# A fourth token pair in the seven-product output projection of a fused attention-plus-gated-unit kernel

## The chip, the cores and the metric

The kernel runs on one core of one Trainium2 chip. The core has five engines that matter here: TensorE (PE in the profile, PEld its weight loads) multiplies matrices into PSUM, VectorE (DVE), ScalarE (ACT) and GpSimd (POOL) do the elementwise work, and SyncE (SP) only issues DMAs. Each engine works through its own queue in order, and waits where a semaphore says that an input isn't there yet. The metric is the device time of one execution in microseconds; before the change it is 214.34, the median of three runs (214.32 to 215.28).

## The reference

For 2,048 tokens of width 512, the kernel adds three terms: the input, a linear attention with learned feature maps (32 heads of 16), and a gated unit with 1,792 hidden columns. Both branches read the layer-normalised input.

```python
xn = _layernorm(x, axis=-1)
return x + _A_ref(xn, A_wqkv, A_w_phi, A_wo) + _B_ref(xn, B_w_gate, B_w_up, B_w_down)

# A: phi = [softmax(q @ w_phi), softmax(-(q @ w_phi))], the same for k
kv = einsum("bhsf,bhsd->bhfd", phi_k, v);  z = sum of phi_k over the tokens
o = (phi_q @ kv) / (phi_q . z + 1e-6);     A = o @ wo
# B
h = (xn @ w_gate) * (xn @ w_up);           B = h @ w_down
```

## The kernel before

The tokens are cut into 16 tiles of 128, and these into four groups T = 0 to 3 of four tiles. Each group has a tile `hT(T)` of hidden values, with the hidden columns on the partitions: 14 chunks of 128 by 512 tokens.

*Gated unit, first half.* Group 0 is computed plainly: the steps `g` and `u` (14 each, lines 348 and 437) are four matmuls of 512 columns, `gc` copies the gate out of PSUM, `h` multiplies. Groups 2 and 3 together, and the two halves of group 1, are computed by block products (line 802): the product of a 2 by 2 block matrix of tokens with one of weights is made from seven products instead of eight, from sums of blocks made beforehand. `z` and `Nz` make the token sums, `t` the weight sums, `p1` to `p7` the products, `k1` to `k3` copy PSUM to SBUF, `j` and `d4` join them into hidden values; in odd blocks `m` multiplies gate by up. Steps with an `N` ahead belong to group 1 and have 256 columns, those without have 512.

*Attention.* For tile n, `vk` and `k` project to values and keys, `kx`/`ky` are the two exponentials on ScalarE, `kr` sums and `ki` inverts them on VectorE, `kp` multiplies on GpSimd, `kv` accumulates on TensorE; `q`, `qx` to `qp` are the same for queries. `qt` turns the result by a DMA, `ab` multiplies with the accumulated state, `de`, `rd`, `ot` divide, `oT` turns again by a DMA. `a` is the layer norm of one tile and `xt` the DMA that turns it; `wq` is the DMA that turns the query weights. All these DMAs are issued on SP, in one queue.

*Output projection.* A plain tile (`fin_steps`, line 662) takes nine steps `f` of two matmuls with 512 columns: 14 chunks of `hT` with `w_down`, and four of the attention output with `wo`; `fs` scales, adds the input, and `fo` stores. Tile 12 is cut by columns in 384 (`f12`) and 128 (`F12`). The six tiles 9, 10, 11 and 13, 14, 15 are instead taken in pairs (n, n + 4) by `pair_steps` (line 936): seven block products over seven chunks each, with 256 columns. Their token sums `S` (`hidden_sum`, line 925) are made on VectorE or GpSimd from `hT(2)` and `hT(3)`, three tiles (384 columns) at once. `P1a` to `P7b` are the products (four and three matmuls), `P2w`, `P3w`, `P8w`, `P4w` the attention part (four matmuls each), `K` the copies out of PSUM, `A` and `B` additions, `J` the last join that writes the output tile, `X` the store. `c` and `w` steps (`ct`, `cb`, `wt`) prepare `w_down`.

*What sets the order.* The whole order is written out by hand in the string `ORDER`, one word for each step; a suffix `/v`, `/g` or `/a` puts a step on VectorE, GpSimd or ScalarE. The loop at line 1060 issues the words one after the other. The string `SLOTS` names the buffer that each step takes out of its ring. `=k`, `=ab`, `=f` and `=ab2` change the use of the two PSUM banks that are not in the general ring of six; they serve here as marks. Between `=k` and `=ab` lie most of group 0 and the key side of the attention; between `=ab` and `=ab2` lie all block products of the gated unit; behind `=ab2` lie the pairs. The same loop adds a wait: after a VectorE step with both operands in SBUF (`z`, `t`, `S`, `m` and the like), the next GpSimd step waits until it is done.

Of the kernel before, what the change touches and what calls it, by code (L numbers as in the profile page):

```python
# [20 lines left out]
def _bcast_ap(ap_in: bass.AP, new_ap):  # L21
# [4 lines left out]
g3 gc3/a =k g1 gc1/a fk2 fk0 g0 u3 fkv2/v fkv0/v fka2/a fka0/a k1 ky1 kx1 u0 gc0/v h3 k0 u1 k2 h0 kr1 h1 ki1 kx0  # L26
ky0 kr0 s6 s5 ky2 n1.0 g4 g6 gc4/a u6 g7 n0.5 kx2 gc6/a gc7/a s7 k3 kp1/g s4 sc4 kx3 n1.6 n0.6 ky3 u7 h7 h6 a5/g
# [27 lines left out]
Np2.5 q10.0 Np4.4 m3.3/g k3.5/a Nk1.5/a p5.5 p4.5 Np6.5 Nj2.5 qi9 j7.5 Nm2.5/g t32/g d4.4/a Nd4.4/a Np5.4 Nj7.4
p1.6 Nk2.5/a Np7.5 Nk3.5/a q10.1 t33/v d4.5 Np3.4 wr2 Nj3.4 wf2 k1.6/a p3.5 Np4.5 up51/a Nd4.5 p6.6 Np1.6
Nk1.6/a Np2.6 qx10 j2.6 k2.6/a qp9/g j3.5 Np5.5 Nj7.5 m7.5/v m3.5/v t40/v t41/g q12.0 p5.6 Np6.6 q12.1 p7.6
Nk2.6/a Np3.5 Np7.6 Nj2.6 Nj3.5 qy10 wp2 qp13/g k3.6/a p1.7 p1.8 Nk3.6/a qx12 k1.7/a Np5.6 Np4.6 p2.7 j7.6 p3.6
p4.6 Nm7.5/g Nd4.6/a oT4 qr10 Nj7.6 Np1.7 qy12 p2.8 p6.7 Np3.6 k1.8/a Nk1.7/a j3.6 k2.7/a Np6.7 j2.7 Nk2.7/a
d4.6/a q14.0 q14.1 Np7.7 Nj3.6 j2.8 Np2.7 p7.7 Nk3.7/a qx14 Np2.9 Nm3.5/v m2.7/v t42/v Nj2.7 k3.7/a Np4.7 qy14  # L60
Np5.7 Nd4.7 p5.7 Nj7.7 t43/g Np2.8 Np1.8 p4.7 Np3.7 j7.7 Nm2.7/g Nm7.7/v Nj3.7 Nm3.7/v Nk1.8/a Np6.8 Nk2.8/a
p1.9 d4.7 p3.7 k1.9/a Np7.8 Np5.8 p6.8 m7.7/g qt13 fo3 qt8 j3.7 p2.9 Nk3.8/a Np4.8 Nd4.8/a k2.8/a p1.10 Nj7.8
Nj2.8 Np3.8 m3.7/g Np1.9 j2.9 Nk1.9/a k1.10/a t50/v ws2 Nj3.8 S1.0/g p6.9 p2.10 Nj2.9 j2.10 Np6.9 p7.8 Np5.9
p5.8 k2.9/a m2.9/v p7.9 Nk2.9/a t52/v k3.8/a j7.8 Np7.9 Nk3.9/a t51/g p5.9 p1.11 p4.8 Nj7.9 p3.8 k3.9/a p4.9
t53/g p6.10 Np4.9 Np3.9 Nm2.9/v j7.9 d4.8/a j3.8 m7.9/g qi10 k1.11/a Nd4.9 p6.11 p3.9 Nj3.9 up61/a t60/v d4.9
Nm7.9/g qp10/g k2.10/a Np1.11 p2.11 j3.9 p7.10 k2.11/a k3.10/a j2.11 Np1.10 p5.10 j7.10 Nm3.9/g m2.11/g m3.9/v
# [9 lines left out]
f4.3 Nj3.13 =ab2 ab8 qy11 ct2.3/g S0.1/v de8/v rd8 ot8 qi15 f4.7 f6.5 f5.2 Nm3.13/g f4.4 f5.0 ct2.0/g ab9 f7.5
S0.2/v Nm7.13/v S2.6/g de9/a rd9 ot9 S2.2/v S2.3/v F12.3 f6.6 f4.8 F12.1 f7.6 wt2.0/v S1.1/g S1.5/g qt14 qt10
qp15/g qt12 m7.13/v oT8 f4.0 j3.13 f7.3 f4.6 F12.2 f5.8 fs4 fs6 ab14 f5.7 de14/a ct1.1/a rd14 oT9 fo0 ot14
S0.6/v m3.13/v f5.1 f5.4 qr11 qi11 f8.8 oT14 f12.5 F12.6 f8.3 fs7 f5.5 f5.3 F12.5 f12.2 ab12 f8.2 P1b.10 de12/a
wt1.1/g wt2.2/g P1a.10 f5.6 f8.7 cb21.0/a f8.5 f8.4 F12.0 K1.10/v S2.1/v rd12 ot12 f12.6 qt15 fo6 P1a.11 f12.1  # L80
ab13 f12.4 P1b.11 oT12 qp11/g fs5 fo7 fo4 fo5 qt11 wt2.1/g ct3.0/a de13/a rd13 ot13 S1.2/v cb22.1/v S1.6/v f8.0
P1a.9 f12.0 P1b.9 f8.1 S3.0/v wt2.3/v S2.5/v wt4.1/v oT13 f12.3 F12.7 f12.7 f12.8 S3.6/v fs12 K1.11/a S2.0/v
ab10 F12.8 ct3.1/a F12.4 cb21.1/a de10/a K1.9/a A1.9/v wt3.1/v P6a.10 f8.6 wt4.0/g P6a.9 P6b.9 K6.9/a cb22.0/a
A6.9/g S3.5/g wt4.3/g S3.4/g P6a.11 P5a.10 P5b.10 Fs12 P6b.10 K6.10/a P2a.9 P2w.9 K5.10/a fs8 P5a.9 rd10 ot10
ab15 wt3.0/v P7a.9 P5b.9 P8w.10 fo12 fo8 oT10 Fo12 K5.9/a de15/v wt4.2/v P7b.9 P2b.9 J2.9 rd15 ot15 K7.9/a
P7a.10 P7b.10 P4w.9 P6b.11 S3.1/g K7.10/v P3b.9 P4a.9 P4b.10 P4w.10 ab11 B6.9/v A7.10/g oT15 K6.11/a A1.10/v
# [6 lines left out]
SLOTS = {  # L93
    "vt": "012341234",
    "s": (
        "012345120345120345120345120435102450321520512405314021341502135024310345243502145102135454351355"
        "425302541532024524343410323514235230251021324153450341245530305230145023201532"
    ),
    "x": (
# [20 lines left out]
def kernel(  # L120
# [896 lines left out]
    t0 = 1  # L1017
# [93 lines left out]
```

## Time and profile before

| | us |
|---|---|
| median of three runs | 214.34 |
| the profiled execution, its own time | 215.05 |
| its span, first to last instruction | 213.3 |
| mean granted TensorE clock (share of full) | 0.998 |

The profiled execution is 0.71 us above the median, and 1.75 us of its own time lie outside the span. In the rows of the profile a line reads: where in the code, engine, operation, output and inputs by name, shape and type, how often; then the busy time, the mean duration of one in nanoseconds, and the idle time of that engine just before, with what ended it. A chain row reads: start in us, length in us, what. A window row gives the busy time of each engine in that stretch, with the number of instructions in brackets.

### The profile page before, as it was taken

How to read it: one execution, taken by the hardware profiler on the slowest of the kernel's cores; microseconds unless marked ns; L12 is line 12 of the kernel's file. 1: busy time of each engine (PE TensorE's matmuls, PEld its weight loads, DVE VectorE, ACT ScalarE, POOL GpSimd, SP SyncE). 2: the span in 40 equal slices, each digit the busy share in tenths (PEclk: the TensorE clock that was granted, in tenths of full speed). 3: DMA queues.
4: the chain of work that ended last, by engine and by line, in shares of the span. 5: the costliest groups of instructions: out<-in, count | busy, mean ns of one | idle time of the engine just before them, and what ended most of it. 6: DMA issues, size and time to landing. Idle time of an engine off the chain costs nothing.

```text
span 213.3 us, 4174 instructions
## 1 busy us (share of the span) xinstructions
PE 206.5 (97%) x1452; PEld 117.8 (55%) x1452; DVE 185.3 (87%) x372; ACT 153.2 (72%) x296; POOL 149.8 (70%) x146
## 2 busy tenths in 40 slices
PE   8999999989999899989999999999999999999993
PEld 3555444444554454535656665655555555679983
DVE  5777799979899999979999999999879979796854
ACT  4648899979999799989989898686755502555200
POOL 3613577987897778997889876768868468909610
PEclk9999999999999999999999999999999999999999
DMA  5999999402314035773000001800000095452222
GB/s 158 260 274 383 379 297 177 92 8 33 70 25 77 0 68 105 147 103 77 0 3 0 0 3 32 179 13 3 0 0 0 0 130 119 101 148 75 50 78 74
DMA packets 47253, 19.95 MB, mean 94 GB/s; under 512 B 37504, under 2 KB 46976, under 8 KB 47104
## 3 DMA queue, kind: packets, MB, share of 16 engines
q1 hardware_dynamic: 47232, 19.69, 40.6%
q8 instruction: 11, 0.18, 0.4%
q14 instruction: 10, 0.08, 0.2%
HBM read 8.67 MB, written 2.10 MB: 50 GB/s over the span
## 4 chain that ended last, share of the span: by engine, by line
PE 78%; DMA 9%; DVE 6%; SPq 2%; ACT 1%; POOL 1%; issue 1%; DVEq 0%; ACTq 0%; POOLq 0%
PE sa L824 16%; PE fin L678 15%; PE sc L824 9%; PE k L337 5%; PE q L337 5%; PE da L960 5%; PE pv L337 4%; PE sb L824 4%; DMA wT<-in_A_wqkv_dram 3%; PE u L351 3%; DMA wgu<-in_B_w_up_dram 2%; PE g L351 2%; DMA oT<-otok 2%; PE db L960 2%; PE dd L960 2%; PE dc L960 2%
## 5 line engine op out<-in xcount | busy, mean ns | idle before, releaser
L549 DVE TENSOR_REDUCE sums<-e 128x64 f32<-128x1024 f32 x32 | 38.3, 1198 | 3.0 <-ACT e L537 2.9
L559 POOL TENSOR_TENSOR phik<-e,rs 128x1024 bf16<-128x1024 f32 x16 | 30.8, 1935 | 13.8 <-DVE rs L554 10.4
L678 PE MATMUL fin<-wd,hT 128*128 128x512 bf16 (+2 forms) x154 | 37.1, 359 | 0.0
L559 POOL TENSOR_TENSOR phiq<-e,rs 128x1024 bf16<-128x1024 f32 x16 | 31.5, 1975 | 4.8 <-DVE hT L846 2.7
L824 PEld LDWEIGHTS <-T 128*128 128x128 f16 x224 | 21.9, 98 | 17.4 <-issue 0.5
L846 POOL TENSOR_TENSOR hT<-u_sb,hT 128x256 f16<-128x256 bf16 (+1 forms) x23 | 21.1, 920 | 5.3 <-DVE T L774 3.0
L357 ACT COPY k<-sa 128x512 f32<-128x512 f32 (+1 forms) x42 | 19.5, 483 | 5.6 <-PE sa L824 4.1
L359 ACT ACTIVATE k<-sa 128x512 f32<-128x512 f32 (+1 forms) x41 | 19.7, 494 | 4.9 <-PE sa L824 4.2
L824 PEld LDWEIGHTS <-wgu 128*128 128x128 bf16 x168 | 16.3, 98 | 12.3
L337 PEld LDWEIGHTS <-x 128*128 128x128 f16 x144 | 13.4, 98 | 14.4 <-DMA x<-xn 1.1
L678 PEld LDWEIGHTS <-hT 128*128 128x128 f16 (+1 forms) x154 | 14.0, 98 | 11.8
L337 PE MATMUL pv<-vk,x 128*128 128x512 bf16 x48 | 18.2, 379 | 0.8 <-DMA x<-xn 0.8
L351 PEld LDWEIGHTS <-wgu 128*128 128x128 bf16 x128 | 12.0, 98 | 12.0 <-DMA wgu<-in_B_w_up_dram 0.4
L554 DVE RECIPROCAL rs<-sums 128x64 f32<-128x64 f32 x32 | 17.3, 543 | 1.5
L337 PE MATMUL k<-vk,x 128*128 128x512 bf16 x48 | 18.2, 379 | 0.0
L824 PE MATMUL sa<-ss,T 128*128 128x512 f16 x56 | 16.3, 379 | 0.0
L839 DVE SCALAR_TENSOR_TENSOR hT<-sc,k 128x512 f16<-128x512 f32 (+1 forms) x28 | 15.3, 548 | 1.1 <-PE sc L824 0.9
L359 ACT ACTIVATE wgu<-wgu,up 128x1024 bf16<-128x1024 bf16 x14 | 16.0, 1152 | 0.0
L710 ACT ACTIVATE junk<-wgu 128x1024 bf16<-128x1024 bf16 x14 | 15.0, 1077 | 1.2 <-DMA wgu<-in_B_w_gate_dram 1.2
L843 DVE TENSOR_TENSOR u_sb<-sc,k 128x512 bf16<-128x512 f32 (+1 forms) x28 | 15.0, 545 | 0.6 <-PE sc L824 0.5
L537 ACT ACTIVATE e<-q 128x512 f32<-128x512 f32 x24 | 13.9, 601 | 1.9 <-POOL phik L559 1.4
L351 PE MATMUL u<-xnT,wgu 128*128 128x512 bf16 (+1 forms) x64 | 14.6, 352 | 0.1
(160 smaller groups left out, 495.7 us busy)
## 6 DMA issues: line engine op xcount, KB each, us to landing
out_dram<-o_sb SPq DMA_DIRECT2D x15, 128.0 KB, 1.9
wd<-in_B_w_down_dram SPq DMA_DIRECT2D x1, 1792.0 KB, 15.4
wgu<-in_B_w_gate_dram SPq DMA_DIRECT2D x2, 640.0 KB, 7.0
wgu<-in_B_w_up_dram SPq DMA_DIRECT2D x2, 640.0 KB, 8.2
xall<-in_A_x_dram SPq DMA_DIRECT2D x1, 1024.0 KB, 12.1
xall<-in_A_x_dram SPq DMA_DIRECT2D x4, 128.0 KB, 2.5
vk<-in_A_wqkv_dram SPq DMA_DIRECT2D x2, 256.0 KB, 3.4
wgu<-in_B_w_gate_dram SPq DMA_DIRECT2D x2, 256.0 KB, 5.0
```

What stands on the lines that cost most here:

```text
L337: nc.tensor.matmul(ps, lhsT=xt(n)[:, j, :], rhs=w[:, j, :], start=(j == 0), stop=(j == DC - 1))
L351: nc.tensor.matmul(ps, lhsT=w[:, c, f * P:(f + 1) * P], rhs=xnT[:, c, lo:hi], start=(c == 0), stop=(c == DC - 1))
L357: A.copy(out=dst, in_=src)
L359: A.activation(out=dst, in_=src, func=AF.Identity, scale=scale)
L549: V.tensor_reduce(out=sums[:], in_=ev(), axis=AX.X, op=ALU.add)
L554: V.reciprocal(out=rs[:].rearrange("p a b -> p (a b)"), in_=held.pop((s + "s", n))[:])
L559: eng.tensor_tensor(out=phi[:].rearrange("p g (x f) -> p (g x) f", f=DH), in0=ev(), in1=held.pop((s + "i", n))[:].to_broadcast((P, 2 * H, ...
L678: nc.tensor.matmul(held["fin", n, lo], lhsT=l, rhs=r, start=len(done) == 1, stop=len(done) == FC + DC)
L824: nc.tensor.matmul(mine[bankname], lhsT=ww[:, j, :], rhs=xx[:, j, :], start=start and j == 0, stop=(j == hc - 1), skip_group_check=True)
L839: V.scalar_tensor_tensor(out=h(*to), in0=mine[ps], scalar=gate_scale, in1=mine[kept][:], op0=ALU.mult, op1=ALU.add)
L846: eng.tensor_tensor(out=h(*to), in0=mine["u", i][:], in1=h(*to), op=ALU.mult)
L960: nc.tensor.matmul(mine[ps][:, 0:W], lhsT=l, rhs=r, start=bool(mine.pop((ps, "new"), False)), stop=True, skip_group_check=True)
```

## The change

Tiles 8 and 12 become a fourth pair. `t0` goes from 1 to 0 and `LAST` from 12 to None, so the 27 plain steps of these tiles (nine each of `f8`, `f12` and `F12`, 54 matmuls in all), with their `fs` and `fo`, go, and `P`, `K`, `A`, `B`, `J`, `X` steps for n = 8 come. The sums `S` now cover four tiles, 512 columns. The second tile of each pair is stored in two halves of 256 columns. `KN = 7` and the new conditions on `b` and on the list of units leave the set of other steps as it was, since FH is 7.

```diff
-    for u in range(FC):
+    for u in [*range(FC), *(FC + k + i for i in (0, FH) for k in range(KN, FH))]:
         unit_steps(u)
...
     for b in range(2 * FH):
         block_steps(b, 0)
-        block_steps(b, 1)
+        if b < 2 * KN:
+            block_steps(b, 1)
...
-        for t in (n, m):
-            steps[f"X{t}"] = (lambda t=t: nc.sync.dma_start(out=out_view(t, t + 1)[:, 0, :], in_=mine["o", t][:]), None)
-
-    t0 = 1
-    LAST = 12
+        def store(t, lo, hi):
+            nc.sync.dma_start(out=out_view(t, t + 1)[:, 0, lo:hi], in_=mine["o", t][:, lo:hi])
+
+        steps[f"X{n}"] = (lambda: store(n, 0, D), None)
+        for c in range(2):
+            steps[f"X{m}.{c}"] = (lambda c=c: store(m, c * W, (c + 1) * W), None)
+
+    t0 = 0
+    LAST = None
```

`ORDER` and `SLOTS` are new from end to end: 1,244 words become 1,247. Some stretches of `ORDER`, around the transposing DMAs of tiles 4 to 10 and the last steps:

```diff
-xt5 u4 g12 g11 g13 h4 ki0 u12 g9 u13 a6/g kp0/g gc11/a s9 s11 s10 s8 u11 a4/a xt4 n0.3 gc9/a kr2 gc13/a n0.1 h11
-h13 xt6 wq g10 gc10/a gc12/a kr3 n2.4 u9 h9 ki2 kv0 g5 sc8 a11/g a10/g vk5.0 a8/g xt11 ki3 vk5.1 kp2/g a9/a
-gc5/a a7/a vc5/a s13 h12 kx5 vk4.0 vk4.1 vc4/a kp3/g vk6.0 s14 fq0 xt10 s15 s12 sc12 xt8 xt9 xt7 ky4 kx4 ky5
...
-J3.10 X10 P2a.11 P2w.11 J2.11 X11
...
+n0.0 kr0 sc4 a5/g a7/g a6/g a4/g xt4 g10 h4 g9 u13 h6 h7 xt6 xt5 ki0 g13 gc13/a u9 gc9/a s10 s11 s9 h9 s8 kp0/g
+xt7 n0.5 h13 gc10/a n1.5 kr2 g11 g12 gc12/a g8 u12 h12 gc8/a u10 u8 ki2 sc8 a10/g a8/g xt8 s15 vk4.0 kv0 vk4.1
+s14 gc11/a n1.6 a9/a vc4/a kx4 ky4 kp2/g a11/g vk6.0 vk6.1 kv1 vk5.0 vk5.1 kv2 kv3 s13 s12 h10 xt9 kx6 ky6 kr4
+ki4 sc12 h8 u11 vk7.0 vk7.1 kr6 ki6 n0.2 vc6/a ky5 kp4/g vc5/a kx5 kr5 xt10 n2.4 ky7 kx7 wq h11 ki5 kr7 kv4 n0.1
...
+J8.11 P7a.10 P7b.10 X15.1 P2w.11 P2a.11 J2.11 P3w.11 P3b.11 J3.11 X11 P4b.11 J4.11 X15.0 K7.10/a A7.10/g J8.10
+X14.1 P4b.10 P4a.10 P4w.10 J4.10 X14.0
```

What stands between the marks `=ab` and `=ab2` on VectorE, counted in the two lists (kinds whose number is the same are left out):

| step | before | after |
|---|---|---|
| `m` (512 columns) on VectorE | 8 | 14 |
| `S` on VectorE | 2 | 8 |
| `z` on VectorE | 0 | 2 |
| `qi`, `up`, `wt`, `Nm`, `de` on VectorE | 11, 0, 1, 8, 5 | 12, 1, 2, 9, 6 |
| `d`, `cb`, `Nk`, `Nz` on VectorE | 8, 1, 1, 1 | 7, 0, 0, 0 |
| all steps on VectorE | 184 | 199 |

On GpSimd the same stretch has 11 steps `m` before and 5 after, 6 `S` before and 8 after, and 0 `wt` before and 1 after. On TensorE it has 98 `p` steps before and 97 after, 22 `q` half-steps before and 20 after, and 44 `f` steps before and 46 after. The two `z` on VectorE stood ahead of `=ab` before.

More of the change, by code (lines that the diff above doesn't have):

```diff
@@ L76 @@
[L76 to L85, printed above, removed]
@@ new lines @@
+P1b.9 f5.5 ab9 m7.13/v ct2.3/a wt1.1/v de9/v Nm3.13/v rd9 S1.5/v ot9 S2.6/g f4.5 P1a.9 f5.3 p3.13 f4.1 f7.6 f7.2
+f7.4 ab14 f4.6 qi11 S2.5/v S0.6/v S2.0/v de14/a rd14 j3.13 f7.3 f5.6 f7.8 f4.4 ot14 oT9 f5.2 f5.1 ab12 P1a.11
+de12/a f5.0 K1.9/a fs7 fs4 rd12 ot12 wt2.3/g qt10 oT14 fo2 fo7 cb21.0/a P1b.8 qp15/g wt2.2/g S1.6/v S3.3/g
+P1b.11 P1a.8 ab8 K1.11/v de8/v rd8 f6.7 P6a.9 K1.8/a cb22.1/a cb22.0/a ct3.0/a ot8 wt4.1/v fs6 m3.13/v P6a.11
+P6a.8 P5a.8 ab13 P5b.8 cb21.1/a f5.7 P2w.9 P6b.9 ct3.1/v S3.4/v oT12 fo4 qt15 oT8 fo6 P6b.8 P6b.11 P2a.9 P2b.9
@@ new lines @@
+A1.9/v K5.8/a K6.8/a de13/a wt3.0/v wt3.1/v P7a.8 P7b.8 f5.8 K7.8/a K6.9/a wt4.2/v J2.9 wt4.3/g A1.8/g A6.8/g
+P8w.8 rd13 P5a.9 P4b.8 P4w.8 P7a.9 ot13 fs5 S3.6/v wt4.0/v ab10 oT13 fo5 S3.2/v S3.1/v P2w.8 A7.8/g P4a.8 P2a.8
+P7b.9 J4.8 J8.8 de10/v K7.9/a P1b.10 B6.8/g S3.5/v rd10 A1.11/v ot10 P1a.10 P2b.8 J2.8 oT10 P3w.8 P3a.8 P3b.8
+J3.8 qp11/g qt11 X8 P5b.9 A6.9/v K1.10/a K6.11/v P4w.9 P3w.9 ab15 de15/a rd15 K5.9/a A7.9/g P4b.9 X12.1 X12.0
+B6.9/v ot15 P3a.9 P2b.10 P7a.11 P3b.9 P6a.10 P6b.10 P8w.9 P7b.11 K6.10/v J3.9 P4a.9 P2a.10 ab11 K7.11/a de11/a
@@ L91 @@
+A1.10/v J8.9 J4.9 P5a.10 P2w.10 J2.10 P3w.10 P5b.10 P3a.10 P3b.10 P4a.11 K5.10/a A6.11/g A7.11/g A6.10/g P5a.11
+P5b.11 oT15 rd11 ot11 P2b.11 oT11 P4w.11 B6.10/v J3.10 K5.11/v X13.0 X10 P3a.11 P8w.10 P8w.11 X9 X13.1 B6.11/v
+J8.11 P7a.10 P7b.10 X15.1 P2w.11 P2a.11 J2.11 P3w.11 P3b.11 J3.11 X11 P4b.11 J4.11 X15.0 K7.10/a A7.10/g J8.10
+X14.1 P4b.10 P4a.10 P4w.10 J4.10 X14.0
 """
```

139 lines of the change are left out of this document (68 added, 71 removed).

## The prediction

> **What bounds the kernel now.** I read the busy shares first, then who TensorE waited for, then busy time by stretches, then the chain that ended last.
>
> ```profile
> span 213.3 us, 4174 instructions
> PE 206.5 (97%) x1452; PEld 117.8 (55%) x1452; DVE 185.3 (87%) x372; ACT 153.2 (72%) x296; POOL 149.8 (70%) x146
> ```
>
> TensorE is busy for all but 6.8 us of the span. So the change pays only where it takes matmuls away or a wait of TensorE, and it costs where another engine makes TensorE wait. The second row to keep in mind is VectorE's 185.3.
>
> ```profile
> PE pv L337 <- DMA x<-xn: 0.8, 1, 0.8
> PE warm L377 <- PEq L1095: 0.8, 1, 0.8
> PE fin L678 <- DMA oT<-otok: 0.7, 1, 0.7
> PE kv L590 <- POOL phik L559: 0.6, 2, 0.4
> PE pq L471 <- DMA wT<-in_A_wqkv_dram: 0.3, 1, 0.3
> ```
>
> These are all of TensorE's waits (total, times, longest). Behind the start-up only 2.4 us are there to be won: 0.8 for the turned input of a tile, 0.7 for turned attention output, 0.6 for key features, 0.3 for the turned query weights.
>
> ```profile
> core 0: us, PE busy (x) PEld busy (x) DVE busy (x) ACT busy (x) POOL busy (x), PEclk, DMA share, GB/s
> 100.00:130.00 30.00, 29.96 (x186) 17.92 (x185) 29.36 (x63) 27.75 (x58) 25.68 (x26) 1.00 0.00 1
> 75.50:171.00 95.50, 94.73 (x597) 53.06 (x595) 89.79 (x190) 77.84 (x153) 76.41 (x69) 1.00 0.22 41
> ```
>
> The last row is the stretch between the marks `=ab` and `=ab2`, found by the first and the last `ab` around it. VectorE is busy for 89.8 of its 95.5 us, and for 29.4 of 30 in its densest part, with TensorE full beside it. Here VectorE is the engine next in line.
>
> ```profile
> 31.84 6.46 DMA wT<-in_A_wqkv_dram
> 40.98 2.47 DMA x<-xn
> 66.50 2.10 DVE ss L796
> 68.59 1.14 DVE sums L549
> 72.15 2.23 POOL phik L559 x2
> 74.43 0.43 PE kv L590 x8
> 81.61 2.16 PE fin L678 x10
> 89.45 4.74 DMA oT<-otok
> 200.07 1.53 PE da L960 x14
> 210.15 0.48 DVE o_sb L989
> ```
>
> The chain of waits (start, length, what) shows where these come from. The turn of the query weights stands ahead of that of tile 7 in SP's queue. A token sum `z` of 2.10 us on VectorE delays the key sums, and so `phik` and `kv`. One turn of attention output took 4.74.
>
> **The matmuls.** Ten matmuls of 512 columns take 2.16 us, 0.216 each, and fourteen of 256 take 1.53, 0.109 each. Tile 8 goes with 18 x 0.216 = 3.89; tile 12, cut in 384 and 128, has the same columns, so 3.89 again (an estimate by columns). The new pair has 49 + 16 = 65 matmuls of 256: 7.09. Together **-0.69**. Of TensorE's steps between the marks, one `p` and two `q` pairs of 0.43 go and two `f` pairs come, so -0.43 of it counts there and -0.26 elsewhere.
>
> **Ahead of `=ab`.** In the new list all four layer norms `a4` to `a7` are on GpSimd, `xt7` is fourth in SP's queue, and `wq` is behind `xt10`, past six turns of inputs. What it delays is `fq0`, which now comes behind `vk7`. So the 0.8 and the 0.3 should go. Both `z` leave this stretch, and with them the 2.10 us ahead of `phik`: the 0.6 should go too, 1.7 in all. Against it, nine turns of inputs still share one queue, and a tile behind them can be the next that is late. Bounds are -1.7 and 0; I take **-1.2**, two thirds, as the causes of all three are moved.
>
> **Between the marks.** Here VectorE gets 15 more steps. Their prices:
>
> ```profile
> L846 DVE TENSOR_TENSOR hT<-u_sb,hT 128x512 f16<-128x512 bf16 x10 | 4.7, 475 | 0.0
> L930 DVE TENSOR_TENSOR wgu<-hT 128x384 f16<-128x384 f16 x10 | 4.2, 428 | 0.0
> L796 DVE TENSOR_TENSOR ss<-x 128x1024 f16<-128x1024 f16 x2 | 3.3, 1627 | 0.1
> 125.97 0.75 DVE L846 TENSOR_TENSOR hT<-u_sb,hT 128x512 f16<-128x512 bf16 x2
> 160.01 0.41 DVE L846 TENSOR_TENSOR hT<-u_sb,hT 128x512 f16<-128x512 bf16 x1
> ```
>
> Two products in a row take 0.75 where one takes 0.41, so 0.08 of each duration overlaps the next; I take it off. Six `m` more: 6 x 0.395 = 2.4. `S` has no row at 512 columns; it lies between 0.428 (384 columns) and two times that, and I take the product's 0.475, of the same size and number of operands: 8 x 0.395 less 2 x 0.35 is 2.5. Two `z`: 2 x 1.55 = 3.1. The other nine kinds change by one step each, five up, four down, and I set them to cancel. VectorE has 7.9 us more: 89.8 + 7.9 = 97.7, more than the 94.3 that TensorE needs (94.73 - 0.43). GpSimd loses six `m` and gains little, ScalarE has 77.8 of 95.5; neither decides.
>
> VectorE never gets all of its time. In the densest 30 us it was idle for 0.64, which is 2.0 over the stretch. Against that it may carry work past the mark, because TensorE then has older work to do:
>
> ```profile
> 171.29 1.89 PE L678 MATMUL fin<-wd,hT 128*128 128x512 bf16 x8
> 173.28 1.14 PE L678 MATMUL fin<-wd,hT 128*128 128x512 bf16 x6
> ```
>
> These two rows, 3.0 us, are projections of tiles whose hidden values are done; the new list has `f` steps of such tiles at the same place. So 97.7 + 2.0 - 3.0 = 96.7, **+1.2** on the 95.5. The low end is TensorE's own 94.3 (-1.2), the high end no carry at all (99.7, +4.2). What is late while VectorE is behind are `j` and `d4`: they free the PSUM banks that the next `p` waits for.
>
> **Behind `=ab2`.** The four `J` of the new pair (0.48 each in the chain's last row) replace two long `fs` and a short one; GpSimd loses load. Three stores are added to SP's queue behind the turns of attention output. The last store is half as large:
>
> ```profile
> L1015 SPq DMA_DIRECT2D out_dram<-o_sb x6: 332/336/531, 201.5 to 210.7; - x6
> DMA to landing us min/median/max: 1.7/1.7/1.9
> out_dram<-o_sb SPq DMA_DIRECT2D x1, 32.0 KB, 1.7
> ```
>
> A whole tile lands in 1.7 to 1.9 us and 32 KB in 1.7, so the half saves 0 to 0.2; I take 0. Issuing takes 0.34, for the half before it hidden behind the last eleven matmuls, 1.20 us. Between `ot11` and its reader `P2w.11` the list now has 26 matmuls, 2.8 us:
>
> ```profile
> DMA to landing us min/median/max: 2.4/2.4/4.7
> ```
>
> The usual turn of attention output fits, the longest would be 1.9 late. I take only the -0.26: **-0.3**, between -0.5 and +1.6.
>
> **Sum.** -1.2 + 1.2 - 0.3 = -0.3. On the profiled execution's own 215.05 (span 213.3 and 1.75 around it) that gives 214.75; on the median of the runs shown, 214.34, it gives **214.0**.
>
> **The rivals.**
>
> *A: VectorE's extra work is absorbed.* If the early joins that free banks stay ahead of the products and sums in VectorE's queue, only late readers wait. The stretch is then 94.3 plus the 0.7 for attention output, 95.0: -0.5 - 1.2 - 0.3 = -2.0, so 212.3. For it speaks that 28 us of VectorE's span are idle; against it, only 5.7 of these lie between the marks, 0.64 in the densest 30 us.
>
> *B: VectorE sets the stretch and carries nothing over.* Behind the mark the new list has `P1b.9`, which reads joined rows, among its first steps, and the `S` sums wait in VectorE's queue behind everything late. Then the stretch takes 99.7: +4.2 - 1.2 - 0.3 = +2.7, so 217.0. It decides as soon as VectorE's work there passes 95.5 less its idle time. For it speaks 97.7 against 94.3; against it, the fin rows above.
>
> *C: VectorE and GpSimd get in each other's way.* A product took 0.41 alone, and here 0.92:
>
> ```profile
> 162.40 0.92 DVE L846 TENSOR_TENSOR hT<-u_sb,hT 128x512 f16<-128x512 bf16 x1
> 162.36 0.68 POOL L846 TENSOR_TENSOR hT<-u_sb,hT 128x256 f16<-128x256 bf16 x1
> ```
>
> It ran while GpSimd worked. If half of the 14 more `m`, `S` and `z` meet this, that is 7 x 0.51 = 3.6 more, so 217.6. Against it speaks the mean of 475: 0.07 above 0.41 over ten products.
> [...]
>
> **How the numbers follow.** A difference below 0.5% (1.07 us) can't be told from no change in this kernel. The forecast gets 0.44, A 0.28, B 0.22, C 0.06. A is faster, B and C are slower; of the forecast's own case, which spreads from 213.0 to 215.5, 0.02 falls on the fast side of that bound and 0.01 on the slow one: faster 0.30, same 0.41, slower 0.29. The range runs from just under A to just under B, 212.2 to 216.8; the ends of all bounds at once (210.9, 220.1) are left out.
>
> **What would show it.** Right: no wait for `x`, `wT` or `phik` among TensorE's waits; between the marks 96 to 97.5 us with VectorE busy over 97% and waits of `sa`, `sc`, `sb` for VectorE or ScalarE; the last matmul to the end unchanged. Wrong: VectorE idle for 4 us or more between the marks (A), a stretch over 98 (B), products on VectorE with a mean over 600 ns (C), or a new wait for a turned tile ahead of `=ab` or behind `=ab2`.

## The result, and the profile after

The changed kernel takes 211.85 us (median of six runs, 211.53 to 212.62), the kernel before 214.63 (six runs, 214.24 to 215.28). The ratio is 0.9871, with an interval from 0.9847 to 0.9896: faster by 1.3%, where no change was forecast, and a little below the range. The profiled execution took 211.99.

From the page of the kernel after: the span, and busy time, share of the span and instructions of each engine.

```profile
span 210.3 us, 4230 instructions
PE 205.2 (98%) x1463; PEld 119.8 (57%) x1463; DVE 188.0 (89%) x389; ACT 152.4 (72%) x296; POOL 139.2 (66%) x138
```

TensorE's busy time fell by 1.3 us, its idle time from 6.8 to 5.1. VectorE has 17 instructions more, but only 2.7 us; GpSimd lost 10.6. These are all of TensorE's waits after (total, times, longest):

```profile
PE warm L377 <- PEq L1101: 0.8, 1, 0.8
PE dc L962 <- DVE o_sb L991: 0.4, 1, 0.4
PE pv L337 <- DMA vk<-in_A_wqkv_dram: 0.3, 1, 0.3
```

The four waits behind the start-up that stood in this list before, 2.4 us in sum, are gone. One is new: `dc` waits for a join that writes an output tile.

To see where the 3.0 us of span came from, the span is cut at the two marks, by the first matmul behind each. These are the windows of the kernel before, and below them those of the kernel after (start and end, length, then busy time of each engine with its instructions):

```profile
0.00:74.70 74.70, 71.85 (x512) 35.46 (x513) 62.78 (x110) 62.23 (x122) 49.66 (x56) 1.00 0.64 159
74.70:170.60 95.90, 95.13 (x595) 53.09 (x592) 90.31 (x192) 78.64 (x153) 76.81 (x69) 1.00 0.21 41
170.60:213.30 42.70, 39.51 (x352) 29.25 (x350) 32.18 (x72) 12.38 (x22) 23.32 (x23) 0.99 0.44 97
```

```profile
0.00:72.70 72.70, 71.29 (x513) 35.96 (x514) 63.77 (x115) 61.44 (x120) 52.67 (x58) 1.00 0.63 164
72.70:167.80 95.10, 95.00 (x589) 52.73 (x588) 92.49 (x204) 79.16 (x155) 71.69 (x65) 1.00 0.25 47
167.80:210.30 42.50, 38.96 (x363) 31.09 (x361) 31.71 (x73) 11.77 (x22) 14.88 (x17) 1.00 0.39 84
```

| | forecast | measured |
|---|---|---|
| ahead of `=ab` | -1.2 | 72.7 - 74.7 = -2.0 |
| between the marks | +1.2 | 95.1 - 95.9 = -0.8 |
| behind `=ab2` | -0.3 | 42.5 - 42.7 = -0.2 |

The middle row is where the forecast went wrong in sign. TensorE is busy for 95.00 of the 95.10 us there, only 0.13 less than before; most of the 0.8 is idle time that is gone (0.77 before, 0.10 after), which is about the wait of 0.7 for turned attention output. VectorE has 92.49, only 2.2 more than before where 7.9 were priced, and stays below TensorE. What the added steps cost is seen in its groups between the marks: products `m` (512 and 256 columns), the sums `S` (two rows), the token sums `z` (count, then busy time, mean ns of one), and below them the `m` and `S` of the kernel before in its window:

```profile
L847 DVE TENSOR_TENSOR hT<-u_sb,hT 128x512 f16<-128x512 bf16 x14 | 5.7, 412 | 0.0
L847 DVE TENSOR_TENSOR hT<-u_sb,hT 128x256 f16<-128x256 bf16 x9 | 2.6, 289 | 0.0
L932 DVE TENSOR_TENSOR wgu<-hT 128x512 f16<-128x512 f16 x6 | 2.3, 405 | 0.0
L932 DVE TENSOR_TENSOR wgu<-wgu,hT 128x512 f16<-128x512 f16 x2 | 0.8, 415 | 0.0
L797 DVE TENSOR_TENSOR ss<-x 128x1024 f16<-128x1024 f16 x2 | 1.5, 769 | 0.0
```

```profile
L846 DVE TENSOR_TENSOR hT<-u_sb,hT 128x512 f16<-128x512 bf16 x8 | 3.8, 490 | 0.0
L930 DVE TENSOR_TENSOR wgu<-hT 128x384 f16<-128x384 f16 x3 | 1.3, 437 | 0.0
```

A `z` takes 0.77 us, not 1.63; a product 412 ns, where it was 490 on average.

### The profile page after: what moved, and what is told of

Read it like the earlier page. It is cut to its first block, busy times and chain, and to the rows that moved or that the text cites. A ratio compares the mean times of both kernels' runs of the same rounds, so it can differ in the third digit from the quotient of the medians.

```text
span 210.3 us, 4230 instructions
## 1 busy us (share of the span) xinstructions
PE 205.2 (98%) x1463; PEld 119.8 (57%) x1463; DVE 188.0 (89%) x389; ACT 152.4 (72%) x296; POOL 139.2 (66%) x138
## 4 chain that ended last, share of the span: by engine, by line
PE 92%; DMA 4%; SPq 1%; DVE 1%; issue 0%; ACT 0%; DVEq 0%; ACTq 0%
PE sa L825 18%; PE fin L682 15%; PE sc L825 9%; PE q L337 7%; PE k L337 7%; PE pv L337 6%; PE u L351 6%; PE g L351 6%; PE da L962 6%; PE sb L825 4%; DMA out_dram<-o_sb 2%; DMA vk<-in_A_wqkv_dram 2%; PE dc L962 2%; PE ab L631 2%; PE kv L594 2%; PE dd L962 2%
## 5 line engine op out<-in xcount | busy, mean ns | idle before, releaser
L563 POOL TENSOR_TENSOR phiq<-e,rs 128x1024 bf16<-128x1024 f32 x16 | 30.9, 1935 | 8.4 <-DVE dK L985 1.4
L682 PE MATMUL fin<-wd,hT 128*128 128x512 bf16 x112 | 29.4, 379 | 0.0
L359 ACT ACTIVATE k<-sa 128x512 f32<-128x512 f32 (+1 forms) x42 | 20.4, 493 | 5.0 <-PE sa L825 2.6
L847 POOL TENSOR_TENSOR hT<-u_sb,hT 128x256 f16<-128x256 bf16 (+1 forms) x16 | 13.1, 824 | 7.9 <-DVE wgu L932 4.3
L682 PEld LDWEIGHTS <-hT 128*128 128x128 bf16 (+1 forms) x112 | 10.5, 98 | 9.9
L825 PE MATMUL sa<-ss,T 128*128 128x512 f16 x56 | 15.8, 379 | 0.0
L359 ACT ACTIVATE wgu<-wgu,up 128x1024 bf16<-128x1024 bf16 x13 | 14.9, 1158 | 0.0
L351 PE MATMUL u<-xnT,wgu 128*128 128x512 bf16 (+1 forms) x64 | 14.1, 353 | 0.0
L541 ACT ACTIVATE e<-k 128x512 f32<-128x512 f32 x24 | 13.3, 612 | 0.9 <-PE k L337 0.7
```

The lines of the kernel that those rows point to most:

```text
L351: nc.tensor.matmul(ps, lhsT=w[:, c, f * P:(f + 1) * P], rhs=(x4 if T else xnT)[:, c, lo:hi], start=(c == 0), stop=(c == DC - 1))
L359: A.activation(out=dst, in_=src, func=AF.Identity, scale=scale)
L563: eng.tensor_tensor(out=phi[:].rearrange("p g (x f) -> p (g x) f", f=DH), in0=ev(), in1=held.pop((s + "i", n))[:].to_broadcast((P, 2 * H, ...
L682: nc.tensor.matmul(held["fin", n, lo], lhsT=l, rhs=r, start=len(done) == 1, stop=len(done) == FC + DC)
L825: nc.tensor.matmul(mine[bankname], lhsT=ww[:, j, :], rhs=xx[:, j, :], start=start and j == 0, stop=(j == hc - 1), skip_group_check=True)
```

## The experiments

Names with a b_ are edits of the kernel before, with an a_ of the kernel after. Each was compared with the kernel before on its own chip, so they are compared with each other by their ratios; 0.001 is 0.21 us. The last three columns are from TensorE's timeline: the start of the first `ab`, from there to the ninth group of `ab` (called the stretch below), and from there to the end. These bounds are nearly the marks, but other steps stand between mark and `ab` in the old order than in the new one, so the columns compare kernels of one order, not the two orders.

| kernel | median us | ratio to before (interval) | first `ab` | stretch | rest |
|---|---|---|---|---|---|
| before | 214.63 | 1 | 75.99 | 94.62 | 42.73 |
| after | 211.85 | 0.9871 (0.9847 to 0.9896) | 72.76 | 95.82 | 41.69 |
| b_x7_first | 219.85 | 1.0260 (1.0212 to 1.0308) | 80.84 | 94.21 | 42.92 |
| b_z_late | 215.47 | 1.0040 (1.0017 to 1.0064) | 74.01 | 96.31 | 42.89 |
| b_six_m_vector | 215.72 | 1.0083 (1.0052 to 1.0113) | 74.66 | 95.88 | 43.03 |
| a_six_m_gpsimd | 215.24 | 1.0030 (1.0004 to 1.0056) | 72.84 | 99.01 | 41.13 |
| a_six_s_gpsimd | 212.60 | 0.9937 (0.9912 to 0.9961) | 72.45 | 96.83 | 41.15 |
| a_five_m_vector | 212.24 | 0.9919 (0.9896 to 0.9943) | 72.45 | 96.67 | 41.48 |
| a_gpsimd6 | 215.76 | 1.0078 (1.0050 to 1.0107) | 72.63 | 99.78 | 41.13 |
| a_probe6 | 213.96 | 0.9968 (0.9942 to 0.9994) | 72.98 | 98.03 | 41.14 |
| a_probe12 | 217.00 | 1.0109 (1.0073 to 1.0144) | 72.57 | 101.04 | 41.12 |
| a_z_early | 213.21 | 0.9955 (0.9935 to 0.9974) | 74.08 | 95.82 | 41.59 |
| a_xt7_late | 213.01 | 0.9908 (0.9876 to 0.9939) | 74.40 | 95.83 | 41.55 |
| a_wq_early | 211.60 | 0.9888 (0.9866 to 0.9910) | 72.73 | 95.81 | 41.27 |
| a_three_pairs | 212.44 | 0.9890 (0.9858 to 0.9923) | 72.54 | 95.83 | 42.11 |
| a_x_early | 211.53 | 0.9887 (0.9858 to 0.9915) | 72.79 | 95.84 | 41.14 |
| a_x_wq | 212.23 | 0.9873 (0.9837 to 0.9909) | 72.69 | 95.84 | 41.99 |

The stretch of 95.82 us comes back within 0.02 in seven of these kernels, so a few tenths count there. The first `ab` can't be read as closely in the kernel before: where its front is unchanged (b_six_m_vector) it starts at 74.66 in one profile and 75.99 in the other, as the wait for the turned tile, 0.8 in the profile of before, isn't in that kernel's list of waits, and the other 0.5 was lost ahead of it. So up to 1.3 of the 2.0 us in the first row of the table above can belong to the one execution of before, and not to its order.

### Between the marks: is VectorE the bound?

**Reductions that nobody reads.** Twelve of them are put on VectorE among the `p` steps of the kernel after, and in a second kernel six.

```diff
+    extra = consts.tile([P, 1], F32)
+    for i in range(12):
+        steps[f"probe{i}"] = (lambda: nc.vector.tensor_reduce(out=extra[:], in_=wo[:, 0, :], axis=AX.X, op=ALU.max), None)
```

> The changed kernel with twelve extra reductions of 512 values on VectorE, spread evenly over the products between the marks; their result is used by nothing. At an estimated 0.55 us each they add 6.6 us to a VectorE that is busy for 93.2 of 95.8 there. Rival B (VectorE sets the stretch): the time rises by 5.5 to 6.6 us. Theory (TensorE runs ahead of it on banks and older work, some slack is left): the first 2.6 us and what can be carried past the mark, about 2 us, cost nothing, the time rises by 1.5 to 3.5 us.

> The kernel after with six additional reductions of 674 ns (4.0 us) on VectorE between the marks, half of what the earlier run added (8.1 us, which cost 5.2). If VectorE has some 2 us to spare there and is the bound beyond it: 4.0 less 2 to 3 is 1 to 2 slower than after, 212.9 to 213.9. Rival (every microsecond on VectorE counts, in proportion): 2.6 slower, 214.4 or more.

The rows of the added work, first in a_probe12 and then in a_probe6:

```profile
L1057 DVE TENSOR_REDUCE extra<-wo 128x1 f32<-128x512 bf16 x12 | 8.1, 674 | 0.0
```

```profile
L1057 DVE TENSOR_REDUCE extra<-wo 128x1 f32<-128x512 bf16 x6 | 4.0, 673 | 0.0
```

A reduction took 674 ns; the 0.55 us expected for it is a guess that no run shows. The stretch grew by 5.2 for 8.1 us and by 2.2 for 4.0. From the one to the other that is 3.0 for 4.1, or 0.73 for each microsecond; at this slope, which rests on two kernels, an estimated 1.0 us (4.0 - 2.2/0.73) was free. So VectorE is close behind TensorE in the kernel after. The load that the prediction gave it, 97.7, is 5.2 above the 92.5 measured; by the same slope that is an estimated 3 us longer, and would not have been absorbed. The price was wrong, not the rule that VectorE is next.

**Six products back on GpSimd.** In the kernel after:

```diff
-m2.1/v m2.3/v m2.5/v m3.3/v m3.7/v m7.9/v
+m2.1/g m2.3/g m2.5/g m3.3/g m3.7/g m7.9/g
```

> The changed kernel, with six of the products m on VectorE between the marks (m2.1, m2.3, m2.5, m3.3, m3.7, m7.9) put back on GpSimd, where the kernel before has them. Rival B of the prediction (VectorE's load sets the stretch between the marks): VectorE has 6 x 0.33 = 2 us less to do and the time falls by 1 to 2 us. Theory (VectorE's load is absorbed, and two-input VectorE steps are lengthened by GpSimd steps beside them): no gain; the time stays within 0.5 us or rises by up to 1 us, and the mean of VectorE's products and sums rises from 0.41 towards 0.45.

The stretch is 3.2 longer, and VectorE is busy for as long as in the kernel after (93.4 and 93.2 us of it) with six steps fewer. Two rows of TensorE's waits and one of VectorE's groups in that kernel:

```profile
PE sc L820 <- DVE u_sb L839: 0.9, 2, 0.7
PE sa L820 <- DVE u_sb L839: 0.5, 1, 0.5
```

```profile
L842 DVE TENSOR_TENSOR hT<-u_sb,hT 128x256 f16<-128x256 bf16 x9 | 4.5, 499 | 0.0
```

Nine products of 256 columns that weren't touched went from 289 to 499 ns, and TensorE waits for VectorE. Either the six results are late, or GpSimd's work slows VectorE's.

**Six products on GpSimd that nobody reads** tell these apart. They are put among the `p` steps of the kernel after:

```diff
+    extra = bd[:].rearrange("p c g d -> p (c g d)")
+    for i in range(6):
+        steps[f"probe{i}"] = (lambda: nc.gpsimd.tensor_tensor(out=extra, in0=wo[:, 0, :], in1=wo[:, 1, :], op=ALU.mult), None)
```

> The kernel after with six additional products of 128x512 on GpSimd between the marks, the size of an m, whose result nobody reads (the output stays the same). It tells the two halves of what six m on GpSimd cost (3.4 us) apart. If that cost is the lateness of the product for its reader, these six cost under 1 us: 211.8 to 212.8. If it is contention of GpSimd's work with VectorE's, they cost 2 to 4 us: 214 to 216, with VectorE's products m at a mean over 500 ns instead of 412.

The stretch grew by 4.0. VectorE's groups in that kernel, the products `m`, the weight sums `t`, and below them the joins that read PSUM:

```profile
L843 DVE TENSOR_TENSOR hT<-u_sb,hT 128x512 f16<-128x512 bf16 x14 | 6.5, 469 | 0.0
L843 DVE TENSOR_TENSOR hT<-u_sb,hT 128x256 f16<-128x256 bf16 x9 | 4.5, 505 | 0.0
L771 DVE TENSOR_TENSOR T<-wgu 128x512 f16<-128x512 bf16 x6 | 3.5, 592 | 0.0
L836 DVE SCALAR_TENSOR_TENSOR hT<-sc,k 128x512 f16<-128x512 f32 x14 | 9.5, 676 | 0.1
```

And the groups of the kernel after that answer to the last two:

```profile
L775 DVE TENSOR_TENSOR T<-wgu 128x512 f16<-128x512 bf16 x6 | 2.5, 412 | 0.0
L840 DVE SCALAR_TENSOR_TENSOR hT<-sc,k 128x512 f16<-128x512 f32 x14 | 9.5, 679 | 0.2
```

The same steps of VectorE take 0.8 + 1.9 + 1.0 = 3.7 us longer (6.5 - 5.7, 4.5 - 2.6, 3.5 - 2.5), though none has more to do; those that read PSUM take the same. A result that is late for its reader can't be the cause here, as nobody reads it. That GpSimd's later steps are late by up to 7 us of added work (six of about 1.16) is not excluded; one wait of VectorE for an `m` on GpSimd (1.0 us) is new.

**The cost by itself**, behind the last step of the kernel after:

```diff
+    def alone(i):
+        nc.vector.tensor_tensor(out=W1q[:, 0, :], in0=wo[:, 0, :], in1=wo[:, 1, :], op=ALU.mult)
+    def beside(i):
+        if i % 3 == 0:
+            nc.gpsimd.tensor_tensor(out=W1q[:, 1, :], in0=W1q[:, 0, :], in1=wo[:, 1, :], op=ALU.mult)
+        nc.vector.tensor_tensor(out=W1q[:, 2, :], in0=wo[:, 0, :], in1=wo[:, 1, :], op=ALU.mult)
...
```

> The kernel after with work added behind its last step, whose result nobody reads (the output stays the same), to measure one cost by itself: 12 products of 128x512 on VectorE alone; 12 of the same beside 4 products on GpSimd; 12 VectorE steps with a single operand in SBUF beside 4 products on GpSimd; 12 of these alone. Contention theory: the first 12 take 0.41 each, the second 12 have some that take 1.0 to 1.6, with 4 us or so more in sum, and the steps with one operand take the same beside GpSimd as alone. Rival (no contention; what six more GpSimd products cost was a late reader): all products take 0.41.

Its groups (alone; beside GpSimd; one operand beside GpSimd; one operand alone; GpSimd's own in the second and third), and the shortest, median and longest of the second and third:

```profile
L1059 DVE TENSOR_TENSOR W1q<-wo 128x512 bf16<-128x512 bf16 x12 | 5.1, 424 | 0.4
L1064 DVE TENSOR_TENSOR W1q<-wo 128x512 bf16<-128x512 bf16 x12 | 8.4, 701 | 0.4
L1069 DVE TENSOR_SCALAR W1q<-wo 128x512 bf16<-128x512 bf16 x12 | 7.1, 594 | 0.4
L1072 DVE TENSOR_SCALAR W1q<-wo 128x512 bf16<-128x512 bf16 x12 | 3.5, 293 | 0.4
L1063 POOL TENSOR_TENSOR W1q<-W1q,wo 128x512 bf16<-128x512 bf16 x4 | 4.9, 1224 | 8.1 <-DVE W1q L1059 7.9
L1068 POOL TENSOR_TENSOR W1q<-W1q,wo 128x512 bf16<-128x512 bf16 x4 | 4.6, 1151 | 3.9 <-DVE W1q L1064 3.6
```

```profile
L1064 DVE TENSOR_TENSOR W1q<-wo x12: 418/426/1256, 212.4 to 220.8; 128x512 bf16<-128x512 bf16 x12
L1069 DVE TENSOR_SCALAR W1q<-wo x12: 288/294/1205, 221.1 to 228.4; 128x512 bf16<-128x512 bf16 x12
```

The median is that of a step alone, the longest is as long as GpSimd's step (1.2 us). (The one run took 235.13 us, with the added work at its end.) So it isn't a general slowing: with eight of the twelve at the median, the sums of 8.4 and 7.1 leave an estimated 1.25 and 1.19 us for each of the other four, as many as GpSimd has steps. In the first pair (start, length) VectorE's step starts under GpSimd's, which ends at 213.87, and ends behind it, at 214.14.

```profile
212.60 1.27 POOL L1063 TENSOR_TENSOR W1q<-W1q,wo 128x512 bf16<-128x512 bf16 x1 [7.89 <-DVE W1q L1059]
212.89 1.25 DVE L1064 TENSOR_TENSOR W1q<-wo 128x512 bf16<-128x512 bf16 x1
```

Four GpSimd products cost VectorE 8.4 - 5.1 = 3.3 us. The steps with one operand suffer too (3.6), against what was expected.

**Six sums on GpSimd, and five more products on VectorE**, both in the kernel after:

```diff
-S2.2/v S0.4/v S0.3/v S2.1/v S0.1/v S2.4/v
+S2.2/g S0.4/g S0.3/g S2.1/g S0.1/g S2.4/g
```

> The kernel after with six of the eight sums S between the marks (S2.2, S0.4, S0.3, S2.1, S0.1, S2.4) on GpSimd rather than VectorE. They are needed only by the pairs behind the mark =ab2. If VectorE's load is the bound, 2.4 us less on it make it faster by 1 to 2 us, near 210. If what counts is how late the reader of a step is (theory), S on GpSimd cost little: within 0.7 us of after, 211.3 to 212.6. If any work with two operands in SBUF on GpSimd slows VectorE beside it (contention), 2 to 3 us slower, 214 to 215, like the six products m.

```diff
-m7.1/g m7.5/g m7.7/g m2.9/g m2.11/g
+m7.1/v m7.5/v m7.7/v m2.9/v m2.11/v
```

> The kernel after with the last five 512-column products m (m7.1, m7.5, m7.7, m2.9, m2.11) on VectorE too, so that no such product is left on GpSimd. By the six additional GpSimd products (0.65 us of VectorE's time for each) five fewer give VectorE 3.2 us back and cost it 5 x 0.33 = 1.6: if that is the whole of it, VectorE's busy time falls by about 1.6 and the kernel is 0 to 1.5 us faster than after, 210.3 to 211.8. Rival (the written order decides: a step is late on the engine whose queue was not written for it, as with the same edit in the kernel before): 1 to 2 us slower, 212.8 to 214.

With `S` on GpSimd the stretch is 1.0 longer: less than for `m`, and again not shorter with six steps fewer on VectorE. With five more `m` on VectorE it is 0.85 longer, against both expectations. The estimate of 0.65 us given back for each GpSimd step didn't hold, and the rows of the kernel after say why: its products already take 412 and 289 ns, and the longest of the 23 between the marks takes 442, so there is nothing to give back.

**The same six products, moved in the kernel before:**

```diff
-m2.1/g m2.3/g m2.5/g m3.3/g m3.7/g m7.9/g
+m2.1/v m2.3/v m2.5/v m3.3/v m3.7/v m7.9/v
```

> The kernel before with six of its products m (m2.1, m2.3, m2.5, m3.3, m3.7, m7.9) on VectorE rather than GpSimd, nothing else changed: the mirror of taking them back in the kernel after, which cost 3.4 us. Theory (a product on GpSimd takes 1.2 us and is late for its reader, and slows VectorE beside it, so that moving it is a gain by itself): 1 to 3 us faster than before, 211.5 to 213.5, with VectorE's busy time up by less than the 2.4 us of the prediction's price. Rival (VectorE is the bound there, and six more products of 0.395 are 2.4 us more on it): 2 us slower, 216 to 217. Third way (a gain only in the order written for it): within 0.5 us of before, 214 to 215.

This is slower by 0.8%, as the rival said. Two windows of the stretch between first and ninth group of `ab`, of this kernel and of the kernel before:

```profile
74.66:170.53 95.87, 94.87 (x585) 52.42 (x584) 91.33 (x195) 77.75 (x151) 68.54 (x63) 1.00 0.21 41
```

```profile
75.99:170.61 94.62, 93.85 (x586) 52.51 (x584) 89.03 (x189) 77.35 (x151) 75.53 (x69) 1.00 0.22 41
```

VectorE has 2.3 us more, which is the prediction's price (2.4), and the stretch is 1.25 longer. But it also began 1.33 earlier, and both kernels reach its end at 170.5 to 170.6, so these two profiles alone don't show that the move cost 1.25 here; the time of the runs shows that the kernel is slower. So taking products from GpSimd is no gain by itself. In either kernel the move away from the assignment that its order was written for costs time.

### Ahead of `=ab`

**Tile 7's turn.** In the kernel before its turn and its layer norm are moved ahead of the query weights; in the kernel after it is issued three turns later.

```diff
-a6/g kp0/g
+a6/g a7/g kp0/g
...
-xt6 wq
+xt6 xt7 wq
...
-gc5/a a7/a vc5/a
+gc5/a vc5/a
...
-xt9 xt7 ky4
+xt9 ky4
```

> The kernel before, with the turn of tile 7 (xt7) put ahead of the turn of the query weights (wq) in SP's queue, and its layer norm a7 on GpSimd behind a6; nothing else moves. Theory (the waits ahead of =ab were worth about 1.1 of what the change gained): TensorE's waits for x (0.8) and for wT (0.3) go or shrink, the time falls by 0.8 to 1.2 us. Rival (the transposes only change places, another tile becomes the late one): the wait shows at another tile or at wT, which now starts later, and the time stays within 0.4 us.

```diff
-kp0/g xt7 n0.5
+kp0/g n0.5
...
-xt9 kx6
+xt9 xt7 kx6
```

> The kernel after with the turn of tile 7 (xt7) issued three turns later, behind xt9 rather than behind xt5; its layer norm stays where it is. If its place in SP's queue is what took TensorE's wait for a turned tile away (0.2 to 1.0 us in the kernel before, by execution), the wait comes back: 0.3 to 1 slower than after, with pv or k waiting for x ahead of =ab. Rival (the four early layer norms on GpSimd suffice, any of the turns behind them is in time): within 0.3 of after.

The first kernel is 2.6% slower, against both expectations, and shows what an early layer norm needs besides its place. A row of TensorE's waits there, and one of GpSimd in time (start, length, with the idle time before it):

```profile
PE kv L585 <- POOL phik L554: 5.2, 3, 4.6
```

```profile
34.56 0.77 POOL L513 TENSOR_SCALAR xn<-xall,rstd,nb 128x512 f16<-128x512 bf16 x1 [6.95 <-DMA x<-xn]
```

`a7` writes one of the five buffers that the turns read, and in this order its buffer is still being turned: GpSimd stands for 6.95 us with `kp0` behind it, and TensorE waits 4.6 for `phik`. The waits for `x` and `wT` did go, but the edit didn't test their price. The second edit is cleaner: the first `ab` is 1.6 later. Of this, 0.4 was lost at the start-up, ahead of the edit. The rest doesn't come as a wait of TensorE for the tile, as the theory had it: `vk7` starts at 41.52, against 41.14 in the kernel after, so only those 0.4 later. It comes through ScalarE. A step there that sums squares of weights (`n0.2`) writes one of the same five buffers, and now waits 2.0 us for tile 7's turn to be done with it; the copies and exponentials behind it are late, and TensorE waits for one of them and for a step of VectorE's that waits behind them (by the starts of the matmuls 0.4 and 0.6). ScalarE's step in time, and the two rows of TensorE's waits:

```profile
41.46 1.06 ACT L706 ACTIVATE junk<-wgu 128x1024 bf16<-128x1024 bf16 x1 [2.01 <-DMA x<-xn]
```

```profile
PE k L332 <- DVE hT L366: 0.5, 1, 0.5
PE k L332 <- ACT vt L352: 0.2, 1, 0.2
```

The interval of its ratio touches that of the kernel after, so the whole time alone doesn't decide it.

**The query weights' turn**, moved forward in the kernel after:

```diff
-xt5 ki0
+xt5 wq ki0
...
-kx7 wq h11
+kx7 h11
```

> The kernel after with the turn of the query weights (wq) moved forward in SP's queue, from behind xt10 to right behind xt5, ahead of xt7: its relative place before the change. If wq's place is what made the wait for a turned tile (1.0 us by the starts of the matmuls) go, it comes back: 0.8 to 1.2 slower than after, 212.7 to 213.1, with a wait of kv or pv for x ahead of =ab. Rival (the layer norms of tiles 4 to 7 on GpSimd, all four ahead of the first turn, are what counts): within 0.5 of after.

Nothing changes: the first `ab` starts at 72.73. Where `wq` stands is not what took the wait for a tile away.

**The token sums `z0` and `z2`**, moved behind `=ab` in the kernel before, and back ahead of it in the kernel after:

```diff
-kp13/g z0/v n0.2
+kp13/g n0.2
...
-f2.4 z2/v qx5
+f2.4 qx5
...
-ot2 qt3
+ot2 z0/v qt3
...
-Nz1/v f0.8
+Nz1/v z2/v f0.8
```

> The kernel before, with its two VectorE token sums z0 and z2 moved behind =ab, about where the changed list has them; nothing else moves. Theory: the waits of kv for phik (0.6) ahead of =ab go, the time falls by 0.4 to 0.7 us, and both sums run in 0.8 us instead of 1.2 and 2.1 if no GpSimd step runs beside them. Rival (VectorE between the marks is at its limit, 89.8 busy of 95.5, so what is moved there is paid there): the 0.6 come back as waits of products between the marks, the time stays within 0.3 us or rises.

```diff
-kp13/g q2.1
+kp13/g z0/v q2.1
...
-kv14 q5.1
+kv14 z2/v q5.1
...
-de2 z0/v rd2
+de2 rd2
...
-t01/v z2/v n2.1
+t01/v n2.1
```

> The kernel after with both token sums z0 and z2 back ahead of =ab, z0 behind kp13 and z2 behind kv14, as before the change. If they are what delayed phik and kv (0.9 us by the starts of the matmuls), that wait comes back: 0.5 to 1 slower than after, 212.4 to 212.9. Rival (VectorE between the marks was near its bound, so that 1.5 us less there pay for it): 0.3 to 1 us faster, 210.9 to 211.5.

A row each, the new wait of b_z_late, that of a_z_early, and the group of its two `z`:

```profile
PE sa L819 <- DVE T L769: 1.6, 1, 1.6
```

```profile
PE ab L626 <- DVE KV L594: 1.5, 1, 1.5
```

```profile
L792 DVE TENSOR_TENSOR ss<-x 128x1024 f16<-128x1024 f16 x2 | 2.5, 1262 | 0.0
```

In the kernel before, the wait for `phik` went and the stretch paid 1.7, with the first products late for their weight sums. In the kernel after the sums ahead of `=ab` cost 1.3 there and the stretch is 95.82 in both cases: between the marks the new order carries them for nothing. One `z` takes 1.26 us on average at the old place and 0.77 at the new one.

### The fourth pair, and the stores

**Three pairs in the new order.** Tiles 8 and 12 are plain again, with `t0 = 1`; the 18 steps `f8` and `f12` stand at the places of the pair's products.

```diff
-    t0 = 0
+    t0 = 1
```

> The kernel after without its fourth pair: tiles 8 and 12 are plain again (18 steps f8 and f12 of two matmuls with 512 columns, at the places of the products P*.8), t0 is 1, and the sums S cover three tiles (384 columns). All other words keep their places. TensorE has 36 x 0.213 = 7.68 where the pair had 65 x 0.107 = 6.93. If the fourth pair is worth its columns (theory): 0.5 to 0.9 slower than after, 212.4 to 212.8. Rival (the pair costs more than it saves: eight sums S more on VectorE, four joins and two more stores): 0.3 to 1.5 faster than after, so that the gain came from the new order alone.

The stretch is 95.83. The rest is 0.4 longer than in the kernel after, and 1.0 longer than the 41.1 that five other kernels with four pairs show, about the 0.7 that the columns save. But the rest runs from 41.1 to 42.0 among the kernels with four pairs, and the ratio can't tell this one from the kernel after, so what the pair itself is worth isn't shown. Most of the 2.8 us came from the new order, and not from the pair.

**Earlier stores**, alone and with the query weights' turn:

```diff
-J3.8 qp11/g
+J3.8 X8 qp11/g
...
-qt11 X8 P5b.9
+qt11 P5b.9
...
-J8.9 J4.9
+J8.9 X9 J4.9
...
-P8w.11 X9 X13.1
+P8w.11 X13.1
```

> The kernel after with the stores X8 and X9 issued right behind the joins that fill their tiles (X8 behind J3.8, X9 behind J8.9). In the kernel after, J8.9 and J8.11 wait 3.1 us together for a store out of the same one of the three output buffers, and TensorE waits 0.4 for J8.9. If that wait counts in full: 0.4 faster, 211.4. Rival: the later turns of attention output come later by the issue of the stores (0.5 us each in SP's queue), and it is 0.5 to 1 slower, or nothing changes since the next wait takes its place.

> The kernel after with two edits that each left the time within what can be told: the stores X8 and X9 right behind their joins, and the turn of the query weights right behind xt5. The first took TensorE's wait of 0.4 for a join behind =ab2 away in its profile, the second shortened it to 0. Together they can't win more than that wait: 0 to 0.5 faster than after, 211.3 to 211.9.

The wait that they were to remove, seen from VectorE in the kernel after:

```profile
DVE o_sb L991 <- DMA out_dram<-o_sb: 3.1, 2, 1.7
```

Two joins wait for stores out of three output buffers. With earlier stores the rest is 0.55 shorter in the profile; but the five kernels with 41.1 leave the stores as they are, and the ratio doesn't tell it from the kernel after. With the query weights' turn moved as well, the rest is 41.99, with a wait of `ab` for turned query features (0.7). No version beats the kernel after beyond the intervals.

## Why the prediction was wrong

**The step that failed** is the third term, between the marks: "VectorE has 7.9 us more: 89.8 + 7.9 = 97.7, more than the 94.3 that TensorE needs". VectorE's busy time rose by 2.2, to 92.5, and TensorE set the stretch. The durations show the sizes. Two `z` were priced 2 x 1.55 and took 1.54 in all: the row that gave the price, 1627, is the mean of two that ran beside GpSimd (the one of 2.10 us began at 66.50, under a GpSimd product that ran from 66.11 for 1.94; the other, 1.16 long, at 73.76, under one from 72.44 for 1.94). The second still ran when the stretch of before began, and its whole length stands in the groups there. Six more `m` were priced 2.4 and added 1.8 (14 x 412 against 8 x 490 in the stretch; one of the eight is the product of 0.92 in rival C's rows). `S` was priced 2.5 and added 1.9 (6 x 405 and 2 x 415 against 3 x 437). The other kinds, set to cancel, took 0.5 less by the sum over all groups. This makes 3.7 by durations, and less by busy time, since steps that follow closely overlap: two products in a row take 0.75 us in the kernel after too (at 111.67), where one takes 0.41. The price of a product, 0.395, held in the old order, as b_six_m_vector shows (2.3 for six).

From that price followed the rest of the term: two more microseconds of idle time taken from the densest 30 us, and 3.0 carried over the mark. VectorE at 92.5 is under the 94.3, and rival A's 95.0 us for the stretch met the measured 95.1.

**Rival A** had the right direction, at a chance of 0.28, and the right stretch, in part by luck: it took 0.43 off TensorE's work, where the windows show 0.13, and kept the wait of 0.7 for attention output, which is gone. Its own sign, VectorE idle for 4 us or more, didn't come either: it was idle for 2.6, as near its limit as the forecast's "busy over 97%" had it. Its reason, early joins ahead of the products in VectorE's queue, wasn't tested by itself. What is shown is that no product of VectorE between the marks takes over 442 ns in the new order (918 in the old), and that its VectorE has an estimated 1 us to spare, by the two probes. **Rival B** fell with the same price; with 8.1 us more on VectorE than the kernel after has, the stretch does grow by 5.2. **Rival C** named an effect that the runs show and put it on the wrong side: a product that takes 425 ns alone took up to 1,256 beside GpSimd's in a_beside, but in the new order the mean is 412.

**Ahead of `=ab`** the direction was right and the size too small: -2.0 against -1.2. By the windows TensorE's idle time there fell by 1.4 (74.70 - 71.85 against 72.70 - 71.29), which is inside the bound of -1.7; the other 0.6 is busy time, for which this term had nothing. Two of the three causes count, the place of tile 7's turn (by way of a buffer, in the new order) and that of the token sums; `wq`'s doesn't. The bounds were read from the waits of one execution: of its waits, those for `x` (0.8), `wT` (0.3) and attention output (0.7) aren't in b_six_m_vector's list, so how much of the 2.0 is the order's stays open.

**Behind `=ab2`** the sum came out, -0.2 against -0.3, but in part by luck: it is made of 0.5 less busy time and 0.3 more idle time, where 0.26 and none had been forecast. The turns of attention output were in time. What wasn't foreseen is the wait for stores out of the three output buffers.

What stays open is why each order punishes a change of engines as it does; that could only be seen as a sum over all words.

## What to carry to other kernels

Take the price of a VectorE step from rows where GpSimd is idle (a `z` took 1.63 us on average beside GpSimd in the kernel before, and 0.77 in the kernel after), look at the shortest and longest and not only the mean, and then ask of the new place what stands beside it. With that price compare the engine next in line with the one that bounds the stretch: below it, added work can be free, as the two `z` were here (a stretch of 95.82 us with them and without), and adding work that nobody reads shows how far. In an order written by hand, undo one assignment at a time before crediting it: here a move that looked like the gain was a loss when made alone in the other order.

## What the runs showed of the hardware

In a_beside a VectorE product with both operands in SBUF, 425 ns alone, took up to 1,256 among GpSimd products of 1,224 on average; in the pair shown it started under GpSimd's and ended 0.27 us behind it. A multiplication of one bf16 operand by a number, 294 alone, took up to 1,205 among GpSimd products of 1,151 on average, against the expectation on record. In a_gpsimd6, six GpSimd products more left the joins that read PSUM at 676 ns (679 in the kernel after), while VectorE's products of 256 columns went from 289 to 505. The reductions of a_probe12 and a_probe6, which read SBUF, took 674 and 673 ns on average; these means agree, so no lengthening like that of the products shows, with GpSimd busy for 71.7 of the 101.0 us of that stretch in a_probe12.

The turn of the same tile, issued in the same order, made TensorE wait 0.8 us in the profiled execution of the kernel before, and isn't among the waits of b_six_m_vector's, whose front is the same.
